# A fused forward and backward kernel: five kinds of stores of its last phase move to GpSimd's queue, with four smaller edits beside them

## The chip, the cores and the metric

The kernel runs on one core of one Trainium2 chip, in one launch. The metric is the device time of that launch in microseconds (us), the median of several executions. Engines are called as in the profile: PE (TensorE, matmuls), PEld (its weight loads), DVE (VectorE), ACT (ScalarE), POOL (GpSimd) and SP (SyncE, which here does nothing but issue DMAs). "SPq" and "ACTq" are the DMA issues of SP and ACT. Each engine runs its instructions in the order in which they stand in its program, and an instruction that waits on a semaphore holds those behind it.

## The reference

The input is one sequence of 2048 positions of 512 channels, bfloat16. The forward sum is

```
xn = layernorm(q)
out = q + A(xn, k, v) + B(xn)
A = xn * (longconv(ks * v) + ks * v * D),  ks = causal 4-tap convolution of k along the sequence
B = ((xn @ w_gate) * (xn @ w_up)) @ w_down          hidden width 1376
```

where longconv is a causal convolution over all 2048 positions with one filter per channel, written with FFTs. The kernel must return the output and, for a given `grad_out`, the gradients of q, k, v, the 4-tap filter, the long filter, D, w_gate, w_up and w_down: ten outputs, `out_0` to `out_9`. In the names of the kernel `o0_n` is the output, `o1_n` the gradient of q, `o2_n` of k, `o3_n` of v, `out_4` of the 4-tap filter, `out_5` of the long filter, `out_6` of D, `out_7` and `out_8` of w_gate and w_up, `out_9` of w_down.

## The kernel before, in words

Positions lie as (partition p, row r): position 16 p + r, so 128 partitions times 16 rows of 512 channels. A "pair" below is two rows, a tile of 128 x 1024 bf16, 256 KB.

Up to about 314 us the kernel does the normalisation, the forward transforms, and for eight chunks of 256 positions the hidden layer and its gradient (L512, L518, L532, L548, L555), while a second stream does the products in the frequency domain and half of the way back (L584 to L619). What later stages need goes through DRAM: `HDD` (hidden activations and their two gradients), `GD` (half-inverted signals: 0 for the convolution's output, 1 for its input's gradient, 2 for the filter's gradient), `KS` (the 4-tap result) and `BX` (per position: q + B, and the gradient that came back through B).

The last phase, from L904 on, is a loop with four side streams beside it. The main loop is `dw()` (L1032): for each of the 11 blocks `fb` of 128 hidden units (the last has 96) it makes the gradient of w_down (`down_grad`, L1010: 16 matmuls into `pd`, cast to `od`, stored) and those of w_gate and w_up (L1050: 128 matmuls into `pu`, cast into `og`, stored at L1061 for two blocks together, the last block by itself). Its operands come from `HDD` by a load `hb` (L793, two buffers; asked for two blocks ahead from the middle of `down_grad`) and are turned by PE transposes (`hid_t`, L847), or, for the last three blocks, by a transposing DMA (L808). `dw()` yields six times a block; these places are counted by `n`, and the side streams, a list `sides` of (start, step, generator) at L1177, go one step whenever `n` reaches their next number:

- `inv_y()` (start 0, step 3): finishes the inverse transform. For each four rows it loads `vb` and `kb` (L925, L927, two buffers each), makes `yC` (rows of the convolution's output), then `dd` (L947, the gradient of the convolution's input) and from it `dks` = dd * v (L950) and `kb` = dd * ks (L951), which is the gradient of v and is stored at L952. Its `g` loads from `GD` (L785, two buffers) are asked for one use ahead. After row pair 2 two small DMAs (L955, L956) copy the first three rows of `dks`, one partition further, behind the last. `load_kh()` (L1145) loads `khC`, k and its three shifted rows, three DMAs.
- `dsk_gram()` (start 27, step 2): gradient of the 4-tap filter: `pk` matmuls of `dks` with `khC` (L1073).
- `inv_dk()` (start 35, step 3): gradient of the long filter: `po` matmuls (L989), cast into `o5t`, stored at L996. `o5t` and `khC` share one buffer (tag `o5k`).
- `ew()` (start 10, step 3): elementwise work on DVE. Step one loads `bb` 0 (`load_fin`, L1113, two buffers, from `BX`). After that one step each for `final(0)`, `final(1)`, `bwd(0)`, `final(2)`, `bwd(1)`, ... `final(7)`, `bwd(6)`, `bwd(7)`. `final(b)` (L1116) asks for the next `bb`, makes the output pair `o` (L1124, L1125, stored at L1126) and the gradient of q, `e` (L1128 to L1140, stored at L1141), with one buffer each of `o`, `e` and `dxn`. `bwd(b)` (L1095) makes the gradient of k, `dk` (two buffers), from four rows of `dks`, seven DVE operations, and stores it at L1107.

A scheduler puts the instructions of each engine in order by their place in the program, moving one ahead of another where it reckons that the other is not ready; operations in a `high_priority` block count as some 300 instructions earlier. `issue_after(ins)` keeps the DMAs of its block behind `ins` on SP. In the trace SP's order in this phase is nearly that of the program: stores of `kb`, `o`, `e` and `dk` stand among the loads.

All DMAs of the phase are issued by SP, save the last `BX` store (L560) and one half of the last `od` (L1027), which ACT issues. POOL does two memsets (L954 and L1147, at 321.54 and 322.97 us) and nothing after them.

Of the kernel before, what the change touches and what calls it, by code (L numbers as in the profile page):

```python
# [8 lines left out]
BF = mybir.dt.bfloat16  # L9
# [9 lines left out]
D = 512  # L19
F = 1376  # L20
R = 16
P = 128
NC4 = 4
# [167 lines left out]
def kernel(  # L191
# [24 lines left out]
    nc = tc.nc  # L216
# [411 lines left out]
    def seq(*its):  # L628
        for it in its:
            for _ in it:  # L630
                yield
# [291 lines left out]
    def load_vk(r0):  # L923
        vb = c2b.tile([P, 2, D], BF, name="vb")
        nc.sync.dma_start(vb[:], v_n[:, r0:r0 + 2, :])  # L925
        kb = c2b.tile([P, 2, D], BF, name="kb")
        DKS["kb", r0] = nc.sync.dma_start(kb[:], KS[:, r0:r0 + 2, :])  # L927
        return vb, kb
# [2 lines left out]

    def inv_y():
        gq = pend
        todo = [(sg, r0) for r0 in range(0, R, 4) for sg in (0, 1)][2:]
        for r4 in range(0, R, 4):
            gy = gq.pop(0)
            vk = [load_vk(r4), load_vk(r4 + 2)]
            for i in range(0, 4, 2):
                st1p(gy, i, yC[:, r4 + i:r4 + i + 2, :])
            if todo:  # L940
                gq.append(load_g1(*todo.pop(0)))
            yield
            gd = gq.pop(0)
            for i in range(0, 4, 2):
                r0 = r4 + i
                vb, kb = vk.pop(0)
                dd = c2b.tile([P, 2, D], BF, name="dd")  # L947
                st1p(gd, i, dd[:])
                with tc.high_priority(offset=SOON):
                    nc.vector.tensor_tensor(dks[:, r0:r0 + 2, :], dd[:], vb[:], op=ALU.mult)  # L950
                    nc.vector.tensor_tensor(kb[:], dd[:], kb[:], op=ALU.mult)  # L951
                DKS[r0] = nc.sync.dma_start(o3_n[:, r0:r0 + 2, :], kb[:])  # L952
                if r0 == 2:
                    nc.gpsimd.memset(dks[96:128, R:R + 3, :], 0.0)  # L954
                    nc.sync.dma_start(dks[0:112, R:R + 3, :], dks[1:113, 0:3, :])  # L955
                    nc.sync.dma_start(dks[112:127, R:R + 3, :], dks[113:128, 0:3, :])  # L956
            if todo:
                gq.append(load_g1(*todo.pop(0)))
            if r4 == R - 8:
                load_kh()  # L960
            yield

    def load_gk(rq):
# [13 lines left out]
    def inv_dk():  # L977
        o5t = c2.tile([P, NC4, P, R], BF, name="o5t", tag="o5k")
        o5 = out_5.rearrange("(c q) s -> c q s", q=P)
        for rq in range(4):  # L980
            gk = gks.pop(0)
            if rq == 0:
                gk_last = load_gk_last()
            for b in range(2):
                po = P2("po", [P, 2, 4, P])
                for h in range(2):
                    for i in range(4):
                        for c in range(2):
                            nc.tensor.matmul(po[:, h, i, :], lhsT=(gk_last(c, i) if rq == 3 else gk[:, c, i])[:, cs(2 * b + h)], rhs=TB.IW[:, c, :],  # L989
                                             start=(c == 0), stop=(c == 1))  # L990
                act(o5t[:, 2 * b:2 * b + 2, :, 4 * rq:4 * rq + 4], po[:].rearrange("q h r s -> q h s r"))
                if b == 1 and rq < 2:
                    gks.append(load_gk(2) if rq == 0 else None)
                if rq == 3:
                    for c in (2 * b, 2 * b + 1):
                        nc.sync.dma_start(o5[c], o5t[:, c].rearrange("q s r -> q (s r)"))  # L996
                yield
            if rq == 0:
                yield from put_dD(o5t)
# [32 lines left out]
    def dw():  # L1032
        og = None
        load_hb(2)
        for fb, (f0, fw) in enumerate(FBLK):
            last = fb + 1 == NFB
            if not last:
                down_grad(fb)
                yield
                hid_t(fb + 1, 0)  # L1040
                hid_t(fb + 1, 1)
                yield
                yield
            pu = P2("pu", [P, NC4, 2, P])
            if fb % 2 == 0:
                og = c2.tile([P, 2, NC4, 2 * P], BF, name="og")
            q0 = (fb % 2) * P
            for c in range(NC4):
                for r in range(R):
                    nc.tensor.matmul(pu[:, c, :, :fw], lhsT=xnC[:, r, cs(c)], rhs=nat_d(fb, r),  # L1050
                                     start=(r == 0), stop=(r == R - 1))
                if c == 1:
                    yield
                    if fb + 1 in TURNED:
                        last_t(fb + 1)
                    yield
            act(og[:, :, :, q0:q0 + fw].rearrange("p t c f -> p c t f"), pu[:, :, :, :fw])
            if fb % 2 == 1 or last:
                a = f0 - q0
                for t, o in enumerate((out_7, out_8)):  # L1060
                    nc.sync.dma_start(o[:, a:f0 + fw].rearrange("(c p) f -> p c f", p=128), og[:, t, :, :q0 + fw])  # L1061
            yield
            if last:
                down_grad(fb)
                yield
# [29 lines left out]
    def bwd(b):  # L1095
        rb = slice(2 * b, 2 * b + 2)
        dk = c2b.tile([P, 2, D], BF, name="dk")
        t = c2.tile([P, 2, D], BF, name="tk", tag="dxn")
        for j in range(4):
            src = dks[:, 2 * b + j:2 * b + j + 2, :]  # L1100
            w = skb[:, j:j + 1, :].to_broadcast((P, 2, D))
            if j == 0:
                nc.vector.tensor_tensor(dk[:], src, w, op=ALU.mult)
            else:
                nc.vector.tensor_tensor(t[:], src, w, op=ALU.mult)  # L1105
                nc.vector.tensor_tensor(dk[:], dk[:], t[:], op=ALU.add)  # L1106
        nc.sync.dma_start(o2_n[:, rb, :], dk[:])  # L1107

    FL = {}

# [5 lines left out]
    def final(b):  # L1116
        if b + 1 < 8:
            load_fin(b + 1)
        bb = FL.pop(b)
        rb = slice(2 * b, 2 * b + 2)  # L1120
        tt = nc.vector.tensor_tensor
        stt = nc.vector.scalar_tensor_tensor
        o = c2.tile([P, 2, D], BF, name="o0")
        tt(o[:], xnC[:, rb], yC[:, rb], op=ALU.mult)  # L1124
        tt(o[:], o[:], bb[:, :, 0, :], op=ALU.add)  # L1125
        nc.sync.dma_start(o0_n[:, rb, :], o[:])  # L1126
        e = c2.tile([P, 2, D], BF, name="e")
        tt(e[:], goC[:, rb], yC[:, rb], op=ALU.mult)  # L1128
        dxn = c2.tile([P, 2, D], F32, name="dxn")
        for i in range(2):  # L1130
            r = 2 * b + i
            stt(dxn[:, i], e[:, i], 1.0, bb[:, i, 1, :], op0=ALU.mult, op1=ALU.add, accum_out=s1[:, r:r + 1])  # L1132
            stt(e[:, i], dxn[:, i], 1.0, xnC[:, r, :], op0=ALU.mult, op1=ALU.mult, accum_out=s2[:, r:r + 1])  # L1133
        nc.vector.tensor_scalar(m2[:, rb], s2[:, rb], -1.0 / D, None, op0=ALU.mult)
        stt(m1[:, rb], s1[:, rb], -1.0 / D, rstd[:, rb], op0=ALU.mult, op1=ALU.mult)
        for i in range(2):
            r = 2 * b + i
            stt(dxn[:, i], xnC[:, r, :], m2[:, r:r + 1], dxn[:, i], op0=ALU.mult, op1=ALU.add)  # L1138
            nc.vector.tensor_scalar(e[:, i], dxn[:, i], rstd[:, r:r + 1], m1[:, r:r + 1], op0=ALU.mult, op1=ALU.add)
        tt(e[:], e[:], goC[:, rb], op=ALU.add)  # L1140
        nc.sync.dma_start(o1_n[:, rb, :], e[:])  # L1141

    KH = []

    def load_kh():  # L1145
        khC = c2.tile([P, R + 3, D], BF, name="khC", tag="o5k")
        nc.gpsimd.memset(khC[0:1, 0:3, :], 0.0)  # L1147
        with tc.issue_after(LG["g"].ins):
            nc.sync.dma_start(khC[:, 3:3 + R, :], k_n)
            nc.sync.dma_start(khC[1:113, 0:3, :], k_n[0:112, R - 3:R, :])  # L1150
            nc.sync.dma_start(khC[113:128, 0:3, :], k_n[112:127, R - 3:R, :])
        KH.append(khC)

    def every(gen, start, step):
        return [start, step, gen]
# [6 lines left out]
    tail.append(lambda: bwd(7))  # L1162

    def ew():
        with tc.issue_after(DKS[2].ins):
            load_fin(0)
        yield
        for f in tail:
            f()
            yield  # L1170

    def load_dk():
        gks.append(load_gk(0))
        gks.append(load_gk(1))
        yield

    sides = [every(seq(inv_y(), load_dk()), 0, 3), every(dsk_gram(), 27, 2), every(inv_dk(), 35, 3), every(ew(), 10, 3)]  # L1177
    for n, _ in enumerate(dw()):
        for sd in sides:
            if n >= sd[0]:  # L1180
# [35 lines left out]
```

## Time and profile before

| | us |
|---|---|
| median of 3 runs | 488.59 (487.62 to 489.19) |
| the profiled execution | 490.11 |
| its span, first to last instruction | 488.3 |
| PE / DVE / ACT / POOL busy | 471.2 / 342.7 / 310.0 / 14.1 |
| last phase, 320 to 480: PE busy | 157.2 of 160 |
| DMA share and GB/s, 350 to 385 | 1.03, 383 |
| DMA share and GB/s, 385 to 395 | 0.51, 185 |
| DMA share and GB/s, 420 to 480 | 0.73, 200 |

Times within an execution are counted from the span's start. A timeline line reads: start, duration, engine, source line, operation, destination <- source, shapes, count, and in brackets the idle time of the engine before it with what ended it. A wait line reads: engine and line that waited, what it waited for, total us, how often, longest. The DMA share is the mean busy share of the core's 16 DMA engines. When each DMA landed is read in the trace from the semaphore that it raises.

### The profile page before, as it was taken

Reading aid. Unit: us, or ns where it says so; the run is one execution under the profiler, and the core shown is the slowest. Engines: PE = TensorE matmul, PEld = TensorE weight load, DVE = VectorE, ACT = ScalarE, POOL = GpSimd, SP = SyncE. Lnnn points to the kernel's source line nnn. Section 1 sums busy time; section 2 is a strip of 40 time slices with the busy share of each in tenths; the row PEclk is TensorE's granted clock in tenths of the full one; section 3 lists DMA queues with packets and bytes.
Section 4 is the critical chain, followed back from the end, with each engine's and each line's share of the span. In section 5 each row is a group of like instructions: output and inputs, shape, how many; then the busy total and the mean of one; then the engine's idle time right before and its main releaser. Section 6 shows DMA issues by size and latency. Waiting matters only on the chain.

```text
span 488.3 us, 10511 instructions
## 1 busy us (share of the span) xinstructions
PE 471.2 (96%) x4335; PEld 314.4 (64%) x4335; DVE 342.7 (70%) x625; ACT 310.0 (63%) x351; POOL 14.1 (3%) x30
## 2 busy tenths in 40 slices
PE   8998999999999999999999999999999899999993
PEld 7866755557548457357357634577677678777791
DVE  6879979977285667667686883030279699998880
ACT  4866677669468678689689954567657524733220
POOL 8000000000000000000000000020000000000000
PEclk9999999999999999999999999999999999999998
DMA  9999999989998878788877299989999789599727
GB/s 274 374 360 355 320 287 330 327 287 327 308 292 290 216 238 255 241 262 249 279 238 244 72 369 311 374 314 337 338 397 361 287 300 388 182 294 241 225 73 243
DMA packets 105838, 139.88 MB, mean 286 GB/s; under 512 B 33435, under 2 KB 78912, under 8 KB 104126
## 3 DMA queue, kind: packets, MB, share of 16 engines
q1 hardware_dynamic: 104206, 137.85, 86.2%
q10 hardware_dynamic: 1584, 1.36, 1.0%
q8 instruction: 34, 0.56, 0.5%
q14 instruction: 14, 0.11, 0.1%
HBM read 68.45 MB, written 63.41 MB: 270 GB/s over the span
## 4 chain that ended last, share of the span: by engine, by line
PE 54%; DVE 23%; DMA 19%; issue 2%; ACT 1%; SPq 1%; ACTq 0%; DVEq 0%
PE px L555 14%; PE pgu L512 13%; PE py L548 6%; PE pdh L518 6%; DMA out_dram<-o 6%; PE ps L584 3%; PE pf L370 3%; DMA ssk<-in_A_ssm_k_dram 3%; PE pg L613 3%; DVE tk L1105 2%; DVE dk L1106 2%; PE pu L1050 2%; DVE dxn L1138 2%; DVE dxn L1132 2%; DVE e L1133 2%
## 5 line engine op out<-in xcount | busy, mean ns | idle before, releaser
L555 PE MATMUL px<-WT,hd 128*128 128x512 bf16 (+1 forms) x352 | 81.0, 380 | 0.0
L1050 PEld LDWEIGHTS <-xnC 128*128 128x128 bf16 x704 | 67.1, 98 | 8.8 <-issue 0.9
L555 PEld LDWEIGHTS <-hd 128*128 128x128 bf16 (+1 forms) x352 | 32.8, 98 | 44.4 <-issue 7.7
L1050 PE MATMUL pu<-natd,xnC 128*128 128x256 bf16 x512 | 58.5, 273 | 0.2 <-ACT nath L235 0.2
L235 ACT CAST gu<-pgu 128x1024 bf16<-128x1024 f32 (+1 forms) x48 | 45.4, 946 | 16.6 <-PE pgu L512 16.2
L235 ACT CAST GO<-pg 128x1024 bf16<-128x1024 f32 x48 | 46.2, 1015 | 13.8 <-issue 7.2
L235 ACT CAST SP<-ps 128x1024 bf16<-128x1024 f32 x47 | 45.6, 1026 | 13.7 <-PE ps L584 11.8
L512 PE MATMUL pgu<-xt,Wu 128*128 128x256 bf16 (+1 forms) x352 | 53.1, 274 | 0.9 <-DVE kn L238 0.6
L600 DVE TENSOR_TENSOR T<-SP 128x2048 bf16<-128x2048 bf16 x24 | 29.4, 1224 | 34.8 <-ACT SP L235 34.7
L512 PE MATMUL pgu<-xt,Wg 128*128 128x256 bf16 (+1 forms) x352 | 52.8, 273 | 0.4 <-DMA Wg<-in_B_w_gate_dram 0.4
L518 PE MATMUL pdh<-gt,WdT 128*128 128x256 bf16 (+1 forms) x352 | 46.9, 273 | 0.1
L235 ACT CAST fst<-pf 128x1024 bf16<-128x1024 f32 x44 | 42.8, 1032 | 5.3 <-PE pf L373 1.8
L235 ACT CAST og<-pu 128x1024 bf16<-128x1024 f32 (+1 forms) x11 | 10.9, 993 | 51.1 <-PE pu L1050 28.1
L512 PEld LDWEIGHTS <-Wu 128*128 128x128 bf16 (+1 forms) x352 | 33.0, 100 | 15.2 <-issue 10.3
L548 PE MATMUL py<-Wd,hd 128*128 128x512 bf16 (+1 forms) x176 | 41.4, 380 | 0.0
L235 ACT COPY natd<-pt 128x2048 bf16<-128x2048 bf16 x16 | 30.0, 1874 | 13.3 <-PE pt L847 13.3
L518 PEld LDWEIGHTS <-WdT 128*128 128x128 bf16 (+1 forms) x352 | 34.9, 100 | 4.8 <-ACT WdT L235 0.2
L512 PEld LDWEIGHTS <-Wg 128*128 128x128 bf16 (+1 forms) x352 | 34.8, 100 | 4.3 <-DMA Wg<-in_B_w_gate_dram 0.7
L533 DVE TENSOR_TENSOR hd<-gu,dh 128x1024 bf16<-128x1024 bf16 (+1 forms) x48 | 30.8, 643 | 0.8
L532 DVE TENSOR_TENSOR hd<-gu 128x512 bf16<-128x512 bf16 (+1 forms) x48 | 19.1, 398 | 16.0 <-ACT gu L235 16.0
L1014 PE MATMUL pd<-goC,nath 128*128 128x512 bf16 x128 | 30.1, 379 | 0.0
L548 PEld LDWEIGHTS <-hd 128*128 128x128 bf16 (+1 forms) x176 | 16.5, 98 | 20.8 <-issue 3.1
(176 smaller groups left out, 692.4 us busy)
## 6 DMA issues: line engine op xcount, KB each, us to landing
HDD<-hd SPq DMA_DIRECT2D x35, 384.0 KB, 5.4
FD<-fst SPq DMA_DIRECT2D x24, 512.0 KB, 5.7
X<-FD SPq DMA_DIRECT2D x24, 512.0 KB, 5.5
GD<-GO SPq DMA_DIRECT2D x24, 512.0 KB, 3.6
g<-GD SPq DMA_DIRECT2D x11, 1024.0 KB, 9.2
hb<-HDD SPq DMA_DIRECT2D x8, 1344.0 KB, 10.4
bb<-BX SPq DMA_DIRECT2D x8, 512.0 KB, 7.3
BX<-bx SPq DMA_DIRECT2D x7, 512.0 KB, 5.1
```

The costliest lines, as they stand in the source:

```text
L235: nc.scalar.copy(o, i)
L370: nc.tensor.matmul(pf[:, c, :], lhsT=TB.W1[:, c, :], rhs=src[:, i, :], start=True, stop=not point)
L512: nc.tensor.matmul(pgu[:w, i, t, :], lhsT=W[:, c, f0:f0 + w], rhs=xt[:, :, c, :], start=(c == 0), stop=(c == NC4 - 1))
L518: nc.tensor.matmul(pdh[:w, i, :], lhsT=WdT[:, c, f0:f0 + w], rhs=gt[:, :, c, :], start=(c == 0), stop=(c == NC4 - 1))
L532: nc.vector.tensor_tensor(hd[:fw, fb0:fb0 + n, 0, :], gu[:fw, :n, 0, :], gu[:fw, :n, 1, :], op=ALU.mult)
L533: nc.vector.tensor_tensor(hd[:fw, fb0:fb0 + n, 1:3, :], gu[:fw, :n], dh[:fw, :n].unsqueeze(2).to_broadcast((fw, n, 2, 256)), op=ALU.mult)
L548: nc.tensor.matmul(py[:], lhsT=hd[:fw, fb, 0, ss], rhs=Wd[:fw, fb, :], start=(fb == 0), stop=(fb == NFB - 1))
L555: nc.tensor.matmul(px[:], lhsT=hd[:fw, fb, t, ss], rhs=W[:fw, fb, :], start=(t == 1 and fb == 0), stop=(t == 2 and fb == NFB - 1))
L584: nc.tensor.matmul(ps[32 * q:32 * q + 32, a, :], lhsT=TB.EF[64 * a:64 * a + 64, 4 * g + q, ri].rearrange("p k j -> p (k j)"), rhs=X[64 * a ...
L600: tt(W[:].rearrange("p c a d -> p c (a d)"), A[:, i:i + 1].rearrange("p c a d -> p c (a d)").to_broadcast((P, 2, 2 * D)), B[:].rearrange(" ...
L1014: nc.tensor.matmul(pd[:fw, :], lhsT=nat_h(fb, r), rhs=goC[:, r, :], start=(r == 0), stop=(r == R - 1))
L1050: nc.tensor.matmul(pu[:, c, :, :fw], lhsT=xnC[:, r, cs(c)], rhs=nat_d(fb, r), start=(r == 0), stop=(r == R - 1))
```

## The change

Seven edits, all in the last phase:

1. The stores of `kb` (L952), the two copies of `dks` (L955, L956) and the stores of `dk` (L1107), `o` (L1126) and `e` (L1141) are issued by GpSimd instead of SP.
2. `e` has two buffers.
3. `ew()` starts at place 4 instead of 10; its first load, `bb` 0, is kept behind the latest `g` load instead of the `kb` store of row pair 2.
4. `khC`'s tile is made, and its first row cleared by POOL, at the start of `inv_y()`.
5. `khC`'s loads are asked for with the last four rows' `vb` and `kb` loads, three places later, and kept behind the last `kb` load instead of the latest `g` load.
6. The last block's `og` takes a buffer of the tag `dd` (two buffers, last used by `inv_y()`) instead of the one `og` buffer.
7. `DKS[r0]` no longer keeps the `kb` stores.

```
     def inv_y():
         gq = pend
+        khC = c2.tile([P, R + 3, D], BF, name="khC", tag="o5k")
+        nc.gpsimd.memset(khC[0:1, 0:3, :], 0.0)
+        KH.append(khC)
...
             vk = [load_vk(r4), load_vk(r4 + 2)]
+            if r4 == R - 4:
+                load_kh()
...
-                DKS[r0] = nc.sync.dma_start(o3_n[:, r0:r0 + 2, :], kb[:])
+                nc.gpsimd.dma_start(o3_n[:, r0:r0 + 2, :], kb[:])
                 if r0 == 2:
                     nc.gpsimd.memset(dks[96:128, R:R + 3, :], 0.0)
-                    nc.sync.dma_start(dks[0:112, R:R + 3, :], dks[1:113, 0:3, :])
-                    nc.sync.dma_start(dks[112:127, R:R + 3, :], dks[113:128, 0:3, :])
+                    nc.gpsimd.dma_start(dks[0:112, R:R + 3, :], dks[1:113, 0:3, :])
+                    nc.gpsimd.dma_start(dks[112:127, R:R + 3, :], dks[113:128, 0:3, :])
...
-            if r4 == R - 8:
-                load_kh()
...
-                og = c2.tile([P, 2, NC4, 2 * P], BF, name="og")
+                og = c2b.tile([P, 2, NC4, P], BF, name="og1", tag="dd") if last else c2.tile([P, 2, NC4, 2 * P], BF, name="og")
...
-        nc.sync.dma_start(o2_n[:, rb, :], dk[:])
+        nc.gpsimd.dma_start(o2_n[:, rb, :], dk[:])
...
-        nc.sync.dma_start(o0_n[:, rb, :], o[:])
-        e = c2.tile([P, 2, D], BF, name="e")
+        nc.gpsimd.dma_start(o0_n[:, rb, :], o[:])
+        e = c2.tile([P, 2, D], BF, name="e", bufs=2)
...
-        nc.sync.dma_start(o1_n[:, rb, :], e[:])
+        nc.gpsimd.dma_start(o1_n[:, rb, :], e[:])
...
     def load_kh():
-        khC = c2.tile([P, R + 3, D], BF, name="khC", tag="o5k")
-        nc.gpsimd.memset(khC[0:1, 0:3, :], 0.0)
-        with tc.issue_after(LG["g"].ins):
+        khC = KH[0]
+        with tc.issue_after(DKS["kb", R - 2].ins):
...
-        KH.append(khC)
...
     def ew():
-        with tc.issue_after(DKS[2].ins):
+        with tc.issue_after(LG["g"].ins):
             load_fin(0)
...
-    sides = [..., every(ew(), 10, 3)]
+    sides = [..., every(ew(), 4, 3)]
```

More of the change, by code (lines that the diff above doesn't have):

```diff
@@ L1175, in load_dk @@
         yield
-    sides = [every(seq(inv_y(), load_dk()), 0, 3), every(dsk_gram(), 27, 2), every(inv_dk(), 35, 3), every(ew(), 10, 3)]
+    sides = [every(seq(inv_y(), load_dk()), 0, 3), every(dsk_gram(), 27, 2), every(inv_dk(), 35, 3), every(ew(), 4, 3)]
     for n, _ in enumerate(dw()):
```

## The prediction

> **What bounds the kernel now.** I read the page first, then the waits and the timeline of each engine from 300 us on, where the last phase lies, then the landing of each DMA. The page's first line of busy times says that TensorE (PE) is the bound: 96% of the span.
>
> ```profile
> PE 471.2 (96%) x4335; PEld 314.4 (64%) x4335; DVE 342.7 (70%) x625; ACT 310.0 (63%) x351; POOL 14.1 (3%) x30
> ```
>
> So an edit off PE pays only where PE stands still: in gaps, and after its last matmul. The waits of PE from 300 us on show one gap worth naming:
>
> ```profile
> PE pt L847 <- DMA hb<-HDD: 2.6, 2, 2.3
> ```
>
> (total us, times, longest). The timeline puts the 2.33 us at 384.2 to 386.54: the transposes of block 5 wait for its `hb` load. SP's timeline tells why it was late:
>
> ```profile
> 368.36 0.36 SPq L1126 DMA_DIRECT2D out_dram<-o  x1
> 374.83 0.34 SPq L1141 DMA_DIRECT2D out_dram<-e  x1
> 375.26 0.39 SPq L793 DMA_DIRECT2D hb<-HDD  x1
> ```
>
> The buffer was free at 366.0 (last transpose of block 3's `hb`), but SP issues in order and stood at the `e` store until DVE had written `e`, so the load left 9 us late. All of SP's long waits are of this kind:
>
> ```profile
> SPq L1141 <- DVE e L1140: 25.5, 5, 6.5
> SPq L1107 <- DVE dk L1106: 13.9, 5, 3.9
> SPq L952 <- DVE kb L951: 10.3, 8, 4.6
> ```
>
> The second place is the end, in the timeline from 474 us:
>
> ```profile
> 474.24 0.33 SPq L1107 DMA_DIRECT2D out_dram<-dk  x1
> ...
> 477.51 2.07 SPq L1061 DMA_DIRECT2D out_dram<-og  x2
> 479.23 0.34 PEld L1014 LDWEIGHTS <-nat 128*96 128x96 bf16 x2
> 479.45 0.59 PE L1014 MATMUL pd<-goC,nat 128*96 128x512 bf16 x2
> ...
> 482.74 0.80 ACT L235 CAST og<-pu 128x768 bf16<-128x768 f32 x1 [10.36 <-DMA out_dram<-og]
> 483.43 0.37 ACT L235 CAST od<-pd 96x256 bf16<-96x256 f32 x1
> ...
> 484.65 0.47 SPq L1027 DMA_DIRECT2D out_dram<-od  x1
> ```
>
> PE ends at 480.04; the span ends at 488.3. In between ACT waits to cast the last block's `og`: there is one `og` buffer, and its store, ready when ACT had cast block 9 at 471.5, stood behind the last `dk` store (DVE done 474.2), an `od` and two `o5t` stores and left at 477.51 to 478.29, landing at 482.64. The last `od` cast is queued behind `og` on ACT.
>
> **The change, part by part.**
>
> *Last `og` in the `dd` tag.* Nothing reads `dd` after 391, so ACT's wait goes. Next late on that chain is PE: `pd` done 480.04, ACT `od` 0.37, DVE `od` 0.42 behind it (as now: 483.43, 483.84), 0.39 to SP's issue (DVE ends 484.26, SP 484.65), 3.65 from there to the end (488.3 - 484.65): 480.07 + 0.37 + 0.03 + 0.42 + 0.39 + 3.65 = 484.93. SP must be free at 481.3: its `o5t` and `og` issues took 6.2 us (475.14 to 481.36), were held by `dk`, and can now begin at 471.5 to 472.4. **Gain 3.37 us.** If SP were held until 474.2 as now, the same issues would end at 481.36, the last `og`'s two (0.94 us) at 482.3, and `od` would leave then instead of at 484.65: 2.3 us of the gain be left.
>
> *Stores to GpSimd.* 8 `kb`, 2 `dks`, 8 `o`, 8 `e`, 8 `dk`: 34 issues leave SP. On SP one takes 0.33 to 0.36 us; the trace has no DMA issued by POOL. Below, I bound its issue by SP's 0.33 us, above by POOL's costliest instruction of this phase, the 1.37 us memset of L954. I take the upper one, since it is POOL's own row: 47 us on an engine that is idle after 324.3, so hidden. What queues behind a waiting store is now only other stores. Their landing: 2.05 us (a lone `dk`) to 14.3 (`o` at 368, behind 2.4 MB of `khC`); I take about 4, the page's median for `o`. `o` has one buffer, reused some 13 us after its store, so `o` landing in under 11 us costs nothing; the 9.8 us that DVE waits for it today lie off PE's path anyhow. `e` in two buffers takes away 0.2 us of DVE wait: nothing.
>
> *The `hb` load* can leave at 366.0 and land in the 11.2 us it took, at 377 to 380: PE's 2.33 us go if nothing else is late. Two things can be.
>
> *Begun six places sooner.* `ew` steps every third place, so everything of it is two steps earlier: `bb` 0 leaves behind the second `g` load (326.68) at 327.3, not 346.59; `bb` 1 and 2 and the first two pairs of `o` and `e` come ahead of the `g` load that left at 354.90, landed at 363.40 and was used by PE at 367.48: spare 4.1 us. That is 2 x 0.52 + 4 x 0.26 = 2.1 MB; the windows view gives 383 GB/s at a DMA share of 1.03 for 350 to 385: 5.5 us. The hole that `bb` 0 and the rest can fill is 7% of 320 to 350 (share 0.93): 2.1 us. Net 3.4, plus 0 to 2.1 us if `dk` 0 and two `kb` stores (0.79 MB), on a queue of their own, get served first: landing at 366.8 to 368.9, a stall of 0 to 1.4 us.
>
> *`khC` later.* It must now follow the last `kb` load (some 370, not 363.82), with `hb` and four `vb`/`kb` loads in front. Today all that and `bb` 3 has landed by 391.3. Now `o` 2, `e` 2, `dk` 1 and `o` 3 may come in too: 1.05 MB, 2.7 us, less the 2.1 us of filled hole: 391.9. PE's first `pk` stands at 391.93, or 389.6 without the old stall: up to 2.3 us. The two stalls share one delay, so the larger counts: 0 to 2.3, and 5.8 if both mis-estimates add (2.3 + 1.4 + 2.1). I take 1.5, between none and 2.3, since some of those four stores will leave after `khC`. **Gain on PE 2.33 - 1.5 = 0.8 us.**
>
> *DVE.* From 335 (`bb` 0 landed) it has 108 us of work (its windows from 340 to 480), so even with 17 us of waits it is done by 460, ahead of PE. Its last stores no longer hold anything.
>
> **Sum.** 3.4 + 0.8 = 4.2 us: span 488.3 to 484.1, that execution's 490.11 to 485.9. It lay 1.5 us over the median of the runs shown, 488.59; I take the difference from the median: **484.4 us**.
>
> **Where a page speaks against it.** SP's rows above show waits, not slow transfers. The Trainium skill, "DMA: Bandwidth & Descriptors", section "Issuing engines are not separate DMA queues", says that issuing from several engines saves only issue time on the sequencer, since all run on the same 16 DMA engines. By that alone the 34 issues at 0.33 us save 11 us of SP, which is not the bound, and the sum would be the 3.4 us of the buffer; the rows at 368 to 375 disagree, because order on SP also holds back loads.
>
> **Rivals.**
> 1. *No new stall:* loads have spare enough. 488.59 - 3.37 - 2.33 = 482.9. For: SP sends `hb` 9 us sooner. Against: DMA share 1.03 to 385.
> 2. *Loads late:* stalls of 5.8 us at `g` and `khC` eat the gain: 488.59 - 3.37 - 2.33 + 5.8 = 488.7, within 0.3%. For: spare of only 4.1 us. Against: `khC` out of the way of `hb`.
> 3. *Slower: GpSimd's issue holds DVE.* If each of the 34 stores stops DVE for POOL's 1.37 us, 47 us join DVE's 108 from 335 on; with 5 us of other waits it ends at 495, and a store (3.8 us) and the closing 0.8 give a span of 499.6, 11.3 us more: 499.9. It decides from about 1 us a store: DVE must cast the last `od` at 480.5, so (480.5 - 335 - 108 - 5) / 34. For: DVE is 98% busy in 395 to 420 (24.40 of 25). Against: DVE's rows are single-rate at best for one-tensor operations (L1139: 512 elements in 0.54 us, while the two-tensor L1140 does 1024 in 0.69). The Trainium skill, "SBUF — State Buffer", section "SBUF: two separate sides", says that DVE in a two-port mode and GpSimd lock each other out of a shared port pair for whole instructions, and that a DMA issued by GpSimd then starves for descriptors; by that rule this rival is real only if L1139 ran in such a mode, which its row does not look like, and no run yet shows a GpSimd DMA.
> 4. *The tail stays:* another store or wait holds `od` as long as `og` did: 488.59 - 0.8 = 487.8.
>
> **How the numbers follow.** Forecast 0.46 (own range 483.3 to 487.0), rival 1 0.23, rival 2 0.14, rival 3 0.10, rival 4 0.07. 0.3% (1.5 us) is about what a measurement of this kernel can tell from no change: faster means under 487.1, slower over 490.1. Forecast and rival 1 are faster: 0.69, and 0.01 of rival 4; rival 2 is same in 0.10 and slower in 0.04, rival 4 same in 0.06, rival 3 slower: 0.70, 0.16, 0.14. The range takes in rivals 1, 2 and 4 with about half a us to spare and leaves out rival 3: 482.3 to 489.0.
>
> **What would show it.** Right: no ACT wait for `og` at the end, the last `og` cast before PE ends, PE's end to the span's end 4.9 us instead of 8.3; `hb` of block 5 issued near 366; PE idle before `pq` near 367 or `pk` near 391 of about 1.5 us. Wrong: DVE's 0.69 us rows grow or it ends after PE (rival 3), PE waits of over 3 us for `g` or `khC` (rival 2), or POOL stores landing 10 us after DVE is done.

## The result, and the profile after

The changed kernel takes **513.29 us** (median of 4 executions, 512.21 to 513.63), the kernel before 488.81 (median of 4, 487.62 to 489.19). The ratio is 1.0501, 95% interval 1.0477 to 1.0526: 5% slower. The forecast was 484.4 us, and its range ended at 489.0. The profiled execution took 512.21 us, with a span of 510.3, 22.0 us longer than that of before.

The page's line of busy times, after:

```profile
PE 478.6 (94%) x4335; PEld 317.3 (62%) x4335; DVE 341.1 (67%) x625; ACT 310.6 (61%) x351; POOL 33.0 (6%) x64
```

VectorE (DVE) has the same work as before. PE has the same 4335 matmuls, but they take 7.4 us longer than the 471.2 of before, and its share fell: PE also stands still more. The waits of PE from 300 us on (total us, times, longest):

```profile
PE pt L847 <- DVE kd L1082: 10.4, 2, 9.5
PE pq L920 <- DMA g<-GD: 4.9, 1, 4.9
PE pk L1076 <- DMA khC<-in_A_k_dram: 3.5, 1, 3.5
PE pk L1076 <- DVE dks L955: 2.8, 2, 2.2
```

With 0.7 us of small ones they make 22.3 us, against 3.0 before. The place where the change was to gain did gain: PE's last matmul ends at 506.78 and the span at 510.3, a tail of 3.5 us instead of 8.3, and ACT casts the last `og` at 503.37, after a wait for PE and not for a landing. So the account closes: 19.3 us more of waits, 7.4 of slower matmuls, 4.8 less of tail, 21.9 in all, of 22.0 measured.

The slower matmuls are the granted clock. Three rows of the windows view (busy us of PE, PEld, DVE, ACT, POOL; then the granted clock, DMA share, GB/s):

```profile
370.00:380.00 10.00, 7.77 (x54) 5.39 (x55) 9.93 (x23) 4.41 (x4) 2.36 (x4) 0.66 0.70 267
400.00:410.00 10.00, 6.64 (x57) 4.60 (x58) 7.15 (x13) 0.00 (x0) 1.62 (x3) 0.66 1.05 397
420.00:430.00 10.00, 5.80 (x39) 3.69 (x40) 9.79 (x24) 2.45 (x2) 1.31 (x3) 0.54 0.43 133
```

Each of these goes with one of PE's long waits (4.86, 3.55 and 9.47 us); in 380 to 390 and 430 to 440 the clock is back at 1.00. The wait of 2.33 us in the kernel before left it at 1.00 (380 to 390). The Trainium skill, "TensorE: Matmul & The Clock Gate", section "HAM oscillation — how this bites in real kernels", gives gaps of more than about 3.4 us on PE as what throttles the clock; these four waits agree with that, but shorter waits in run 6 do not (last section). A long wait on PE can so cost more than its own length.

**Where the waits begin.** VectorE's timeline shows it. Before, `dks` and `kb` of rows 4 to 7 run as soon as their `dd` is there:

```profile
343.49 0.69 DVE L950 TENSOR_TENSOR dks<-dd,vb 128x1024 bf16<-128x1024 bf16 x1 [12.91 <-ACT dd L235]
```

After (the same operation is on L955):

```profile
343.51 0.68 DVE L1143 TENSOR_TENSOR e<-e,goC 128x1024 bf16<-128x1024 bf16 x1
350.94 0.69 DVE L1131 TENSOR_TENSOR e<-goC,yC 128x1024 bf16<-128x1024 bf16 x1 [6.74 <-DMA out_dram<-e]
351.55 0.69 DVE L955 TENSOR_TENSOR dks<-dd,vb 128x1024 bf16<-128x1024 bf16 x1
```

An `e` that needs a buffer whose store has not landed now stands ahead of `dks`. GpSimd issued that store at 344.49, as soon as `e` was written, and it landed at 350.81, 6.3 us later, among loads that keep the DMA engines full (DMA share 1.02 from 344.5 to 350.8). VectorE waits for it, and with it everything queued behind. Before, VectorE waited for such landings too (4.13 us at 366.91, 3.69 at 382.72), but behind the `dks` and `kb` of rows 4 to 11, and PE did not come to wait for it.

What comes of it on SyncE, then on PE:

```profile
352.26 0.33 SPq L925 DMA_DIRECT2D vb<-in_A_v_dram  x1
...
358.04 0.34 SPq L927 DMA_DIRECT2D kb<-KS  x1
358.47 0.38 SPq L793 DMA_DIRECT2D hb<-HDD  x1
...
361.41 0.53 SPq L785 DMA_DIRECT2D g<-GD  x1
```

```profile
372.23 3.59 PE L920 MATMUL pq<-g,IW 128*128 128x512 bf16 x8 [4.86 <-DMA g<-GD]
...
404.41 0.64 PE L1076 MATMUL pk<-khC,dks 128*64 128x256 bf16 x4 [2.24 <-DVE dks L955]
...
424.20 1.68 PE L847 MATMUL pt<-ident,hb 128*128 128x128 bf16 x14 [9.47 <-DVE kd L1082]
```

The `vb` load needs the buffer that `dks` frees, the `kb` load the landing of the `kb` store, and `hb` and `g` stand behind both. The `g` load left at 354.90 before and at 361.41 now, and PE waits 4.86 us for it. Later it repeats, on VectorE:

```profile
396.60 0.69 DVE L1127 TENSOR_TENSOR o<-xnC,yC 128x1024 bf16<-128x1024 bf16 x1 [5.70 <-DMA out_dram<-o]
...
403.67 0.68 DVE L955 TENSOR_TENSOR dks<-dd,vb 128x1024 bf16<-128x1024 bf16 x1
...
423.30 0.85 DVE L1082 TENSOR_TENSOR kd<-pk,ident 64x256 f32<-64x256 f32 x2
```

`dks` 12 came at 389.34 before. `kd` at 423.30, behind a row of `o`, `e` and `dk` operations, is what the 9.47 us of PE waited for. Engine by engine, PE's and ACT's operations stand in the same order in both programs; on VectorE and SyncE the operations named here stand in another order.

### The profile page after: what moved, and what is told of

It reads as the page before. It is cut to its first block, busy times and chain, and to the rows that moved or that the text cites. A ratio compares the mean times of both kernels' runs of the same rounds, so it can differ in the third digit from the quotient of the medians.

```text
span 510.3 us, 10529 instructions
## 1 busy us (share of the span) xinstructions
PE 478.6 (94%) x4335; PEld 317.3 (62%) x4335; DVE 341.1 (67%) x625; ACT 310.6 (61%) x351; POOL 33.0 (6%) x64
## 3 DMA queue, kind: packets, MB, share of 16 engines
q1 hardware_dynamic: 99440, 129.07, 77.6%
q0 software_dynamic: 2672, 8.78, 4.6%
## 4 chain that ended last, share of the span: by engine, by line
PE 58%; DMA 16%; issue 15%; DVE 8%; POOL 2%; ACT 0%; SPq 0%; POOLq 0%; DVEq 0%; ACTq 0%
PE px L555 13%; PE pgu L512 12%; PE py L548 6%; PE pu L1053 6%; PE pdh L518 6%; PE pf L370 3%; PE pd L1017 3%; DMA out_dram<-e 3%; PE ps L584 3%; PE pg L613 2%; DMA ssk<-in_A_ssm_k_dram 2%; DMA bb<-BX 2%; DMA hb<-HDD 2%; DMA x_b<-in_A_q_dram 2%; DMA out_dram<-o 1%
## 5 line engine op out<-in xcount | busy, mean ns | idle before, releaser
L555 PEld LDWEIGHTS <-hd 128*128 128x128 bf16 (+1 forms) x352 | 32.8, 98 | 44.4 <-issue 7.7
L1053 PE MATMUL pu<-natd,xnC 128*128 128x256 bf16 x512 | 59.7, 276 | 0.2 <-ACT nath L235 0.2
L235 ACT CAST gu<-pgu 128x1024 bf16<-128x1024 f32 (+1 forms) x48 | 45.4, 946 | 16.6 <-PE pgu L512 16.4
L235 ACT CAST SP<-ps 128x1024 bf16<-128x1024 f32 x47 | 45.6, 1025 | 13.7 <-PE ps L584 11.8
L235 ACT CAST og<-pu 128x1024 bf16<-128x1024 f32 (+1 forms) x11 | 10.9, 993 | 49.8 <-PE pu L1053 49.8
L847 PE MATMUL pt<-ident,hb 128*128 128x128 bf16 x336 | 24.2, 228 | 10.7 <-DVE kd L1082 10.4
L847 PEld LDWEIGHTS <-hb 128*128 128x128 bf16 x336 | 22.0, 103 | 16.0 <-DVE kd L1082 11.4
L1017 PE MATMUL pd<-goC,nath 128*128 128x512 bf16 x128 | 31.7, 394 | 0.0
```

The source lines that it names most:

```text
L235: nc.scalar.copy(o, i)
L555: nc.tensor.matmul(px[:], lhsT=hd[:fw, fb, t, ss], rhs=W[:fw, fb, :], start=(t == 1 and fb == 0), stop=(t == 2 and fb == NFB - 1))
L847: nc.tensor.transpose(pt[:, r, :fw], hs[:, (r % 2) * 128:(r % 2) * 128 + 128], ident[:fw, :fw])
L1017: nc.tensor.matmul(pd[:fw, :], lhsT=nat_h(fb, r), rhs=goC[:, r, :], start=(r == 0), stop=(r == R - 1))
```

## The experiments

Theories. **Order**: with a store on GpSimd the scheduler puts the operations that use the store's buffer again (the next `o`, `e`, `dk`; on SyncE the next `vb` and `kb` load) ahead of `dks`, `kb` and `kd`, and on the chip they stand there until the store has landed. **Early start**: it is the work begun six places sooner that delays `g`, `khC` and `dks`. **The stores themselves**: a GpSimd store lands late, or its issue holds VectorE, whatever the order. All times are medians; ratios are to the kernel before, run on the same chip.

| run | change | us | ratio, 95% interval |
|---|---|---|---|
| 1 | after, start at place 10 | 511.22 | 1.0478 (1.0445 to 1.0510) |
| 2 | after, stores on SyncE | 487.03 | 0.9977 (0.9957 to 0.9998) |
| 3 | before, stores on GpSimd | 511.70 | 1.0507 (1.0464 to 1.0550) |
| 4 | before, last `og` in `dd` | 488.89 | 1.0022 (1.0003 to 1.0042) |
| 5 | run 3, both orders held | 490.09 | 1.0043 (1.0018 to 1.0068) |
| 6 | before, VectorE in the order of run 3 | 501.89 | 1.0268 (1.0227 to 1.0308) |
| 7 | run 3, VectorE's order held | 491.00 | 1.0050 (1.0030 to 1.0070) |
| 8 | run 4, last three stores on GpSimd | 482.42 | 0.9865 (0.9819 to 0.9911) |
| 9 | after, VectorE's order held, SyncE's in part | 491.56 | 1.0087 (1.0059 to 1.0115) |
| 10 | before, last three stores on GpSimd | 482.37 | 0.9899 (0.9868 to 0.9930) |
| 11 | run 2, last three stores on GpSimd | 486.94 | 0.9986 (0.9965 to 1.0008) |
| 12 | run 8, `hb` load moved ahead | 494.30 | 1.0137 (1.0103 to 1.0170) |
| 13 | run 6, SyncE's load order too | 509.19 | 1.0429 (1.0398 to 1.0460) |
| 14 | run 10, `hb` ahead, orders held | 485.71 | 0.9941 (0.9919 to 0.9962) |

### Which part of the change

**Run 1.**

```diff
-    sides = [..., every(ew(), 4, 3)]
+    sides = [..., every(ew(), 10, 3)]
```

> The changed kernel with one edit undone: the final sums begin at place 10 again. Theory A (early start): beginning sooner brings 2 MB of loads and stores ahead of the g load and puts DVE's store-waiting operations ahead of dks; undone, the time falls to 484 to 488 us. Theory B (stores on POOL): the stores' move changes the order of DVE's and SP's programs, so that operations which reuse a buffer of o, e or dk, and loads which reuse a buffer of kb, stand ahead of dks, kb and kd and wait there for stores to land; this stays, so the time stays at 500 to 513 us.

It stays as slow as the changed kernel. PE waits for `kd` 12.5 us, for `dskt` 5.0 and for `khC` 4.0, and for `g` no more. The early start is not the cause of the loss.

**Run 2.** All 34 stores back on SyncE, the rest of the change kept.

```diff
-        nc.gpsimd.dma_start(o1_n[:, rb, :], e[:])
+        nc.sync.dma_start(o1_n[:, rb, :], e[:])
...
```

> The changed kernel with the 34 stores issued by SP again, all else as changed (early start, two e buffers, khC later, last og in another buffer). Theory A (early start): the front-loading stays, 500 to 513 us. Theory B (stores on POOL): DVE's program has dks ahead again, 483 to 489 us: the gain of the last og buffer is there, some load waits on SP stay.

Some 26 us go (513.29 to 487.03). One long wait of PE is left:

```profile
371.18 3.60 PE L920 MATMUL pq<-g,IW 128*128 128x512 bf16 x8 [3.77 <-DMA g<-GD]
```

The granted clock is 0.89 over 350 to 380. This wait is put down to the early start, since it is not there in run 1; no run undoes the start alone with the stores on SyncE.

**Run 3.** The reverse: only the stores move (and `bb` 0 is kept behind the latest `g` load, since its old anchor was a store).

```diff
-        nc.sync.dma_start(o1_n[:, rb, :], e[:])
+        nc.gpsimd.dma_start(o1_n[:, rb, :], e[:])
...
```

> The kernel before with one edit: its 34 stores issued by GpSimd (bb 0, which was kept behind a kb store on SP, is kept behind the latest g load at the same place). Theory A (early start): no harm, 485 to 489 us. Theory B (stores on POOL): slow by itself, 497 to 515 us, with PE waits for g or for kd, while DVE's rows keep their 0.69 us. If GpSimd's descriptors themselves were the trouble, DVE's rows would be longer than 0.69 us or a lone store would land in much over 2 us.

The stores alone cost 23.4 us (511.70 less 488.30). PE's waits:

```profile
PE pk L1073 <- DVE dks L950: 14.2, 2, 13.2
PE pt L847 <- DVE kd L1079: 6.7, 3, 2.8
```

### Order, or the stores themselves

Runs 5 to 7, 9 and 12 to 14 carry a helper that records the instructions of the last phase by source line, on VectorE, SyncE or both, and adds edges that fix the order of issue on that engine (asked for without a semaphore). Engines that are not held stay free to be ordered anew. It moves lines down by 23, and what it records shows its own line, L247.

```diff
+    def hold(rec, lines, off):
+        at = {l: iter(v) for l, v in rec.got.items()}
+        prev = None
+        for l in lines:
+            i = next(at[l + off])
+            if prev is not None:
+                tc.add_manual_dep(i, prev.name, mybir.DependencyInfo(mybir.DependencyClass.NoSync, mybir.DependencyReason.DATA), reason="hold")
+            prev = i
...
+    hold(vec, [1124, 1128, 950, 951, 950, 951, ...], 23)
+    hold(sy, [793, 785, 785, 793, 793, 1022, ...], 23)
```

**Run 5.** Run 3, with both lists in the order of the kernel before.

> The kernel before with its 34 stores issued by GpSimd, as in the run that took 511.7 us, but with ordering edges that put the last phase's VectorE operations and SyncE's remaining DMAs in the order that they have in the kernel before. Nothing is added but the order. Theory 'order' (a store on GpSimd makes the scheduler put operations that reuse a store's buffer ahead of dks, kb and kd): the loss of 23 us goes, 485 to 490 us, PE waits for dks and kd under 3 us in all. Rival 'the stores themselves' (a GpSimd store lands later or slows its neighbours, whatever the order): 505 to 512 us, DVE waiting for landings as in that run.

21.5 of the 23.4 us are gone (490.09 is 1.9 over its 488.15), with every store still on GpSimd. VectorE still waits for landings, but PE's waits for `dks` are gone and those for `kd` are down to 2.0 us:

```profile
DVE e L247 <- DMA out_dram<-e: 7.5, 3, 4.6
PE ptd L1028 <- DVE dskt L238: 4.6, 1, 4.6
PE pt L870 <- DVE kd L247: 2.0, 2, 1.6
```

The 4.6 us for `dskt` is new: that cast stands on VectorE behind an `e` that waited 4.56 us for a landing. The same `e` and the first transposing load, before and in run 5:

```profile
426.25 0.69 DVE L1128 TENSOR_TENSOR e<-goC,yC 128x1024 bf16<-128x1024 bf16 x1 [0.18 <-DMA out_dram<-e]
426.31 5.90 SPq L808 DMA_TRANSPOSE natT<-HDD  x1
```

```profile
430.15 0.69 DVE L247 TENSOR_TENSOR e<-goC,yC 128x1024 bf16<-128x1024 bf16 x1 [4.56 <-DMA out_dram<-e]
419.51 5.42 SPq L831 DMA_TRANSPOSE natT<-HDD  x1
```

Before, SyncE stood at the store of the `e` before this one until 423.08, and it landed in 3.15 us; now GpSimd issues that store at 422.88, when the load is already under way, and it lands 7.25 us later. That the earlier load is what slowed it is read from these times; no run moves it alone. So the 1.9 us is a sum: in the profiled run the tail is 4.8 us shorter than before (3.5), and PE ends 5.5 us later (485.50).

**Run 6.** The mirror image: every store on SyncE, VectorE's list in the order of run 3.

> The mirror image: every store stays on SyncE, but ordering edges give VectorE's operations of the last phase the order that they have with the stores on GpSimd. Theory 'order': slow without one GpSimd store, 500 to 525 us, PE waiting for dks and kd by over 10 us in all; more than 512 is possible, since SyncE's loads now queue behind stores that are ready late. Rival 'the stores themselves': 487 to 490 us, as the kernel before.

13.7 us slower without one GpSimd store. VectorE stands at landings, PE's waits are scattered (10.7 us in all, of which 5.0 for `dks` and `kd`, where over 10 was expected), and the granted clock is 0.84 over 410 to 440:

```profile
DVE o L247 <- DMA out_dram<-o: 19.6, 6, 7.1
PE pk L1096 <- DVE dks L247: 3.2, 1, 3.2
```

This run is not as clean as runs 5 and 7. In its trace PE, which was left free, has 46 matmuls (of `pk`, `pd` and `pu`) at other places than before and than in run 3; how much of the 13.7 us they carry is open.

**Run 7.** Run 3 with VectorE's list alone.

> As the run with both orders held, but VectorE's order alone is held; SyncE's loads keep the order that the scheduler gave them with the stores on GpSimd (vb and kb loads ahead of hb). If VectorE's order carries the loss: 486 to 492 us. If it is SyncE's loads, standing at a kb buffer whose store has not landed: 500 to 511 us, with hb or g late for PE.

491.0 us: VectorE's order is what carries the loss; PE's order is that of run 3. SyncE's loads in their new order do little harm as long as VectorE isn't late.

**Run 13.** Run 6, with SyncE's loads also in the order of run 3.

> Every store on SyncE, VectorE's order and also the order of SyncE's loads as they come out with the stores on GpSimd. VectorE's order alone gave 501.9 us of the 511.7. If the missing 10 us are SyncE's loads, standing at kb buffers ahead of hb: 507 to 515 us. If they come from the stores being on GpSimd (their issue or landing once the order is bad): 500 to 504 us.

509.19 us: 20.6 us of loss with all stores on SyncE, so of the 9.7 us between runs 6 and 3, 6.9 go with the loads' order, which hurts once VectorE is late; PE's order is that of run 6, but for four matmuls. What is left to the stores' own place is 1.9 us on the whole (run 5) or 2.8 (run 3 less run 13). In run 5 that is after the 4.8 us that the tail gains, so the stores' place costs PE more than it shows.

**Run 9.** The whole changed kernel, VectorE in the order of run 2 and SyncE too, save the `vb`, `kb` and transposing loads: the list leaves them free, and they came out in another order.

> The whole changed kernel, its 34 stores on GpSimd, with ordering edges that put the last phase's VectorE operations and SyncE's DMAs in the order of the same kernel with its stores on SyncE (487.0 us). Theory 'order': the 23 us go here too: 485 to 491 us, the g wait of some 4 us staying. Rival, that other parts of the change (e in two buffers, the early start) make GpSimd's stores cost something by themselves: 495 us or more.

The loss falls from 24.5 us (513.29 less 488.81) to 4.2 (491.56 less 487.40) by order. A wait for `khC` (5.1 us) is left, while the one for `g`, which was expected to stay, is 0.8.

So the theory "order" stands: the loss goes with VectorE's order while the stores stay and PE's order stays (run 7), and most of it comes with the order while the stores don't move (runs 6 and 13, with PE's 46 matmuls as said). The landings do not tell the two queues apart: between 335 and 400 us the stores of `o`, `e`, `dk` and `kb` took 3.9 to 10.9 us on GpSimd (after) and 2.1 to 14.3 on SyncE (before). Why the scheduler orders them so is inside it; that it reckons a GpSimd store done sooner is a guess from where it puts the next user, and no run shows it.

### The tail and the `hb` load

**Run 4.** The kernel before with the last `og` alone changed.

```diff
-                og = c2.tile([P, 2, NC4, 2 * P], BF, name="og")
+                og = c2b.tile([P, 2, NC4, P], BF, name="og1", tag="dd") if last else c2.tile([P, 2, NC4, 2 * P], BF, name="og")
```

> The kernel before with one edit: the last block's og takes a buffer of the tag dd. All theories: ACT's 10.4 us wait at the end goes, the last od leaves some 3 us sooner: 485.2 us (486.5 if SP, still held by the last dk store until 474.2, is late with the last og and od issues). No change beside that.

No gain. The last `og` no longer waits for a store on ACT, but SyncE's timeline shows what holds the end:

```profile
468.48 4.69 SPq L1107 DMA_DIRECT2D out_dram<-dk  x2
473.26 1.42 SPq L1022 DMA_DIRECT2D out_dram<-od  x1
...
482.37 0.79 SPq L1027 DMA_DIRECT2D out_dram<-od  x1
```

SyncE stands at the last `dk` until 472.84. Then ten DMAs, most of them piled up behind it, leave in one run, 9.9 us of issue (473.26 to 483.16) without a pause worth naming, while the DMA share jumps from 0.16 (470 to 475) to 0.96 (475 to 480). PE ends at 477.78, the last `od` leaves at 482.37, the tail is 8.6 us.

**Run 8.** Run 4, and the last `e` and the last two `dk` stores on GpSimd. No buffer is used again after them, and no engine's order changes.

```diff
-        nc.sync.dma_start(o2_n[:, rb, :], dk[:])
+        (nc.gpsimd if b > 5 else nc.sync).dma_start(o2_n[:, rb, :], dk[:])
...
-        nc.sync.dma_start(o1_n[:, rb, :], e[:])
+        (nc.gpsimd if b == 7 else nc.sync).dma_start(o1_n[:, rb, :], e[:])
```

> The kernel before with the last og in another buffer (488.9 us by itself) and only the last three stores of e and dk issued by GpSimd; no buffer is used again after them, and no engine's order changes. If what ate the 3.4 us of the buffer was SyncE's queue (the last e and dk stores hold od, o5t and og until 472.8, which then leave all at once): the end comes 3 to 4 us sooner, 484.5 to 486.5 us. If the end is bound by the bytes of the last og, od and o5t whenever they leave: 488 to 489.5 us.

5.7 us faster than before, more than expected.

**Run 10.** The same three stores, and the last `og` in its old buffer.

> The kernel before with only the last three stores of e and dk on GpSimd; the last og keeps its one buffer. By the reading of the tail as two holds in a row (SyncE held by the last dk store, then the last og held by its buffer) og 8 and 9 leave some 2.5 to 4 us sooner, and so the last og can be cast sooner, but it still waits for their landing: a gain of 1.5 to 4 us, 484 to 486.7 us. If og's buffer alone were the hold: 488 us. If the queue alone were it: 482.4 us, as with both.

The same time as run 8, as the last of the three readings had it: the queue alone is the hold, and the buffer is worth nothing. GpSimd's, ACT's and SyncE's lines of run 10:

```profile
472.87 0.54 POOL L1107 DMA_DIRECT2D out_dram<-dk  x1 [3.78 <-DVE dk L1106]
```

```profile
475.56 0.80 ACT L235 CAST og<-pu 128x768 bf16<-128x768 f32 x1 [4.29 <-PE pu L1050]
```

```profile
479.81 0.34 SPq L1027 DMA_DIRECT2D out_dram<-od  x1
```

With SyncE free, the store of `og` 8 and 9 leaves at 470.37, so its one buffer is free when PE has the last `pu`: ACT waits for PE and not for a landing. The tail is 3.6 us (478.92 to 482.5).

**Run 11.** Run 2 with the three stores on GpSimd, as in run 8.

> The changed kernel with its stores back on SyncE except the last three of e and dk: early start, later khC, e in two buffers and the last og's buffer all stay. The version with all stores on SyncE took 487.0 us and its last dk store did not hold the tail (PE ended 3.2 us before the span). If the g wait of 3.8 us with its slower clock is what is left over: 486 to 487.5 us. If the three stores help here as they did before: 483 to 484.5 us.

No gain over run 2 (487.03): there VectorE was done sooner and its stores no longer held SyncE. Against run 10 it is 4.6 us slower, with 4.0 us of PE wait for `g`: what else the change brings costs as much as the tail gains.

**Run 12.** Run 8 with one change of SyncE's list: `hb` of block 5 ahead of the second `o` and `e` stores.

```diff
+    hold(sy, [..., 1113, 793, 1126, 1141, 1022, ...], 23)
```

Run 8 has 1113, 1126, 1141, 793, 1022 at this place.

> The 482.4 us version (last og in another buffer, last three stores of e and dk on GpSimd) with one SyncE order edited by hand: the hb load of block 5 ahead of the second o and e stores, which kept it until VectorE had written e. If that store order is why hb is late, as the prediction said: hb leaves at 367 to 369 instead of 375.6, PE's 1.9 to 2.3 us wait for it goes, 480 to 482.4 us. If the load lands when it does because the DMA engines are full: no change, 482 to 483.

The load left at 367.04 instead of 375.61 and its wait on PE went. But VectorE's order, left free, changed: `dks` and `kb` of two row pairs came out earlier, the third `e` store was issued at 396.25 instead of 391.95, and the next `hb`, behind it, came late (later PE also waited 3.8 us for `og` on ACT):

```profile
406.00 1.68 PE L870 MATMUL pt<-ident,hb 128*128 128x128 bf16 x14 [5.37 <-DMA hb<-HDD]
```

**Run 14.** Run 10 with the same edit, VectorE's order and the rest of SyncE's held.

> The kernel before with the last three stores of e and dk on GpSimd (482.4 us) and the hb load of block 5 ahead of the second o and e stores, now with VectorE's order and the rest of SyncE's held as in that version. In the free version (494.3 us) the wait for this hb went, and a later one of 5.4 us for the next hb came, behind an e store that VectorE wrote late. If that is the reordering again: the later wait stays away and the first one goes, 480 to 482.4 us. If an earlier hb simply takes the DMA engines from the loads behind it: 483 us or more, with a wait for another load on PE.

`hb` left at 367.40, and PE's wait for `hb` fell from 2.4 us to 0.7. In its place `pk` waits for `dks`, 1.5 us, and the time is not better than run 10's. What came late is not a load but the `o` store right behind `hb` (1.3 MB): it landed 16.6 us after its issue (368.38 to 384.97), in run 10 12.9 (368.87 to 381.80), and VectorE waited for it ahead of `dks`, 5.94 us (2.27 in run 10):

```profile
384.99 0.69 DVE L247 TENSOR_TENSOR o<-xnC,yC 128x1024 bf16<-128x1024 bf16 x1 [5.94 <-DMA out_dram<-o]
```

The `vb` loads behind it landed as before (386.54; run 10: 386.61). This order does not bring the 2.3 us.

## Why the prediction was wrong

**The step that failed** is "What queues behind a waiting store is now only other stores", and with it the terms "47 us on an engine that is idle after 324.3, so hidden" and "`o` landing in under 11 us costs nothing". They were worked out for the order of VectorE's operations in the trace of before, and the working took that order over unchanged. The kernel's text lets the scheduler choose it, and it chose another: the waits for landings are no longer behind `dks` but ahead of it. With the old order held, the stores on GpSimd cost 1.9 us on the whole (run 5); with the new order 23.4 (run 3). Even in the old order "nothing" was too little: run 5 has the shorter tail in it, and against run 10, which moves only the last three stores, it is some 7 us slower. None of the four rivals named the order.

*The rivals.* Rival 3 (slower: GpSimd's issue holds VectorE) has the sign but not the cause. VectorE's operations take 0.69 us as before, its busy time is 341.1 us against 342.7, and held order takes the loss away. The port lock that the Trainium skill names in "SBUF — State Buffer", section "SBUF: two separate sides", was seen in no row here; the L1142 operations, which would have had to be in a two-port mode, kept their 0.5 us each. Rival 2 (loads late) came true in part: run 2's wait for `g` is 3.77 us where "0 to 1.4" was worked out. PE got the data at 371.2, not at 366.8 to 368.9. `khC` cost nothing there, since PE came to it only at 397.16 and it had landed at 393.48; in run 9, with little wait for `g`, it cost 5.1 us, where the working put up to 2.3.

*The tail.* Forecast: a gain of 3.37 us, 2.3 at worst, from the buffer. Measured: the tail shrinks by 4.8 us, but by SyncE and not by the buffer, whose own worth is nothing in runs 4 and 10. ACT's 10.36 us for the landing of `og` in the timeline of before was a wait for a store that had itself been held by the `dk` store. The "2.3 us left" has the last `od` leave 8.1 us after the last `dk` store (474.2 to 482.3); in run 4 it leaves 9.5 us after it (472.84 to 482.37), before the change it was 10.4.

*The `hb` load.* Right as a mechanism (it left at 367.0 when it was put ahead, and its wait on PE went), and the wait went in the changed kernel too (0.2 us left), where PE itself is late. Its size is not steady: 2.3 us in the profile of before, an execution of 490.11 us, and 0.4 in that of run 4, which has the same order on every engine. But it is no gain by itself: something else is late next (runs 12 and 14).

*GpSimd's issue* was put at 1.37 us; it takes 0.54 to 0.81. *The rule against the change.* The Trainium skill, "DMA: Bandwidth & Descriptors", section "Issuing engines are not separate DMA queues", says that another issuing engine saves only issue time. Run 5, where little but the issuing engine differs, is 1.9 us slower, not faster. But run 10 does not agree: three stores of 0.33 us of issue each, moved, gain 5.0 us, because what stood behind them on SyncE no longer waits. The prediction set the rule aside because SyncE's order holds back loads; that held for these three stores and not for the other 31.

## What to carry to other kernels

Where a scheduler orders an engine's program, moving a DMA to another queue can reorder engines that the edit doesn't touch. Before working out what a wait costs, ask what order the changed program has, and treat the order in a trace as part of what the change may alter.

Try first the stores whose buffers are not used again: here three of 34 gave all of the gain. When an engine waits for a landing, look for what held that DMA's issue before giving it a second buffer.

## What was not expected of the hardware

A lone 256 KB store landed 2.36 us after GpSimd issued it (run 10, 468.53 to 470.89) and 2.05 us after SyncE did (before, 469.88 to 471.93). The issue itself takes GpSimd 0.54 us and SyncE 0.33, though VectorE was busy all through. So a lone store took 0.3 us longer from GpSimd here. The profile lists GpSimd's DMAs as a queue of another kind, `software_dynamic`, and in larger packets: 8.78 MB in 2672, where before the same stores made 4766 packets of SyncE's queue (104206 less 99440).

The length of a wait alone did not tell whether the granted clock falls. Windows of run 6:

```profile
409.10:412.40 3.30, 3.30 (x18) 1.82 (x16) 1.29 (x2) 1.87 (x1) 0.00 (x0) 0.50 1.06 440
429.60:436.30 6.70, 5.19 (x48) 5.02 (x48) 5.78 (x12) 3.55 (x3) 0.00 (x0) 0.50 1.05 276
```

A wait of 3.21 us (before 396.70) left the clock at 1.00, as did the 2.33 us in the kernel before. But a wait of 2.01 us (before 408.69) was followed by 0.50, and so were two of 1.10 and 1.15 us (before 427.77 and 429.97). The sentence on 3.4 us in the Trainium skill, "TensorE: Matmul & The Clock Gate", section "HAM oscillation — how this bites in real kernels", does not fit these; what decides is open here.

The price can be worked out for the changed kernel. The clock is 0.50 in 371.2 to 377.8, 401.9 to 408.6 and 418.9 to 429.1; PE is busy in 14.4 us of them. Half of that, 7.2 us, is about the 7.4 us of slower matmuls, on 22.3 us of waits.
